# Two landmark inversions per batch joined into one chain, and projections whose row halves are swapped, in a Nyström attention and two FFN kernel

## The chip, the cores and the metric

One core of one Trainium2 chip runs the whole program. The metric is the device time of one execution in microseconds; of the kernel before, three runs were taken.

## The reference

Attention over 4 batches of 8 heads, 576 tokens, 64 wide; its output, 2304 tokens of 512, passes through two feed-forward layers (512 to 2048 to 512). All in fp32.

```
q_lm, k_lm = means of q, k over 18 neighbouring tokens     # 32 landmarks
A = sm(q, k_lm);  B = sm(q_lm, k_lm);  C = sm(q_lm, k)     # softmax of scaled products
Z = B.T / (max column sum of B * max row sum of B + 1e-6)
6 times: Z = 2 Z - Z B Z                                   # Newton steps
x = A Z C v
x = (h * tanh(softplus(h))) @ w_out,  h = x @ w_in         # layer 1, mish
x = silu(h) @ w_out2,                 h = x @ w_in2        # layer 2
```

## The kernel before

**Attention.** A group is four heads of one batch, so there are 8 groups, two to a batch. Per group, `sums` (L1074) and `main` (L1136) make the landmark means; `main` also makes B (128x32: four heads of 32 landmarks), its softmax, the two norms, and the first Newton product; `c_side` (L1304) makes C v; `a_side` (L1371) makes A with the landmarks on partitions (tile `at`, a high and a low part of 128x576, made by `at<-at,am`, an exponential, `at<-at,ar`, a transpose and a split); `newton` (L1258) carries the tile `yu` (32 columns of Y next to the 64 columns of u = C v) through six steps. In batch 0 a step is 8 matmuls of 32x32 blocks; from batch 1 on, a step first builds `bd`, a block-diagonal matrix, on DVE, then does `t<-yu,bd` on PE and `yu<-yu,t` on DVE. At its end `t<-bd,yu` gives Z C v, transposed, into `ut` (64 wide per head).

**Projections.** w_in of layer 1 isn't applied to the attention's output but folded into Z C v: `projection` (L641) multiplies `ut` of a batch with decoded columns of w_in (`wa`, 128x512) into `wp`. There are 16, four (`fb`, 512 columns each) per batch. One is 8 matmuls `t<-wa,ut` of 64 rows by 32 columns by 512, which the profile counts as 16 since an fp32 matmul has two records; then ACT or DVE copies the high part and DVE subtracts the low part (`wp<-t,wp`).

**Units.** Layer 1 then is 128 units of 6 matmuls `h<-at,wp` (128x288) and 12 `y<-g,wo` (L917, L946). Between them `gated` (L928) makes mish on ACT and DVE and splits it into a high and a low part (`g<-z,g`, 128x288). A unit needs `wp` and `at` of its batch (`h_time`, L1460).

**Weights.** They arrive in packed halves and `decode` (L530) restores fp32: one ACT pass, then a shift and two bit operations on DVE (`wa<-wst,wa`, `m<-wst,m`), then for w_out a high part and a low one (`wo<-m,wo`). Layer 2 works on three token tiles of 768 with seven products each (a Strassen scheme); `inputs` (L683) loads a tile's quarters and adds them on DVE (`wst<-wst`, 128x768).

**Order.** Nothing runs on its own: class `Line` is a planner that walks a clock of its own, with costs per engine, and records every instruction in the order in which it issues them (`issue`, L256; DMAs by SP in `transfer`, L268). Chains (generators) say which engine they want next; `KINDS` holds for each kind of chain a rank, a lead and a gap; `BIAS` shifts the choice where an operation may go to two engines (`split` for the low parts on DVE or POOL). If PE has nothing to do, `cold` (L188) lets the main loop put in fillers, transposes of `ident` whose results nobody reads. On the chip each engine then runs its list in that order and waits where data is late.

## Time and profile before

| | |
|---|---|
| median of 3 runs | 850.13 us (850.02 to 850.81) |
| profiled execution | 849.0 us, span 847.2 us |
| TensorE clock granted | 0.998 (2.4 GHz is 1) |
| first unit starts | 44.97 us |
| first projection of batch 1 | 123.91 us |
| layer 1 ends, layer 2 begins | 460.2 us |

The profile is that of one execution. Times in it count from the start of the span. PE is TensorE's matmuls, PEld its weight loads, DVE, ACT and POOL are the three other engines, SP issues DMAs. `out<-in` names tiles by the program's names without their numbers. The duration of a matmul includes its latency, so what one costs in a stream is the distance of starts.

### The profile page before, as it was taken

What the parts mean: (1) busy time and instruction counts of PE and PEld (TensorE: products, weight loads), DVE (VectorE), ACT (ScalarE), POOL (GpSimd) and SP (SyncE); (2) the same over time, 40 slices, a digit from 0 to 9 for tenths busy, and PEclk for the clock granted to TensorE, in tenths of its full rate; (3) what the DMA queues carried; (4) which work ended last, traced back from release to release, by engine and by line L of the source; (5) the groups of instructions that cost most, each with busy time, mean ns of one, the idle gap of its engine ahead of it and who ended that gap; (6) DMA issues with size and microseconds to landing.
All of it is one profiled execution on the core that took longest, in us unless ns stands there. A gap on an engine that the chain in (4) does not pass through costs nothing.

```text
span 847.2 us, 15580 instructions
## 1 busy us (share of the span) xinstructions
PE 828.9 (98%) x5922; PEld 735.2 (87%) x5922; DVE 532.3 (63%) x1088; ACT 445.1 (53%) x979; POOL 281.8 (33%) x324
## 2 busy tenths in 40 slices
PE   8999999999999999999999999999999999999997
PEld 6687978878899898989899898988888988998885
DVE  7968665664477787434407999877555567555542
ACT  6576765747465655433435665554444444544422
POOL 3323533442345565415333244221223221232210
PEclk9999999999999999999999999999999999999999
DMA  9664114200145465331117223101300000200002
GB/s 297 233 208 132 59 55 141 79 8 30 47 160 185 146 212 176 111 113 52 52 57 226 97 83 107 38 1 50 102 0 1 1 1 11 65 1 1 1 2 74
DMA packets 41483, 72.31 MB, mean 85 GB/s; under 512 B 4288, under 2 KB 30912, under 8 KB 41408
## 3 DMA queue, kind: packets, MB, share of 16 engines
q1 hardware_dynamic: 40832, 70.53, 26.1%
q8 instruction: 46, 0.75, 0.4%
q10 hardware_dynamic: 576, 0.79, 0.3%
q14 instruction: 29, 0.24, 0.1%
HBM read 57.15 MB, written 14.16 MB: 84 GB/s over the span
## 4 chain that ended last, share of the span: by engine, by line
PE 91%; DVE 3%; DMA 2%; ACT 2%; issue 1%; SPq 1%; DVEq 0%; ACTq 0%
PE y L256 49%; PE h L256 32%; PE t L256 10%; DMA wp<-in_q_dram 1%; SPq L268 1%; DVE z L256 0%; ACT z L256 0%; DMA wst<-ys 0%; DMA out_dram<-ysb 0%; DVE wa L256 0%; DVE at L256 0%; DVE nm L256 0%; ACT wp L256 0%; DVE asm L256 0%; ACT ysb L256 0%
## 5 line engine op out<-in xcount | busy, mean ns | idle before, releaser
L256 PE MATMUL y<-g,wo 128*128 128x288 f32 x1536 | 229.6, 300 | 0.0
L256 PEld LDWEIGHTS y<-g,wo 128*128 128x128 f32 x1536 | 209.0, 189 | 12.4 <-issue 11.3
L256 PE MATMUL y<-wo,xg 128*128 128x512 f32 x693 | 179.8, 395 | 0.0
L256 POOL TENSOR_TENSOR g<-z,g 128x288 fp32r<-128x288 f32 x127 | 112.7, 901 | 155.6 <-ACT g L256 114.5
L256 PEld LDWEIGHTS y<-wo,xg 128*128 128x128 f32 x693 | 128.6, 188 | 20.8
L256 DVE TENSOR_TENSOR z<-h,z 128x384 f32<-128x384 f32 x162 | 88.5, 554 | 67.6 <-PE h L256 65.0
L256 PE MATMUL h<-at,wp 128*128 128x288 f32 x768 | 120.8, 302 | 3.9 <-ACT z L256 3.7
L256 PEld LDWEIGHTS h<-at,wp 128*128 128x128 f32 x768 | 106.3, 188 | 12.1 <-ACT z L256 6.2
L256 ACT ACTIVATE z<-h 128x288 f32<-128x288 f32 x128 | 51.8, 413 | 70.4 <-PE h L256 65.6
L256 ACT ACTIVATE z<-z 128x384 f32<-128x384 f32 x94 | 49.4, 525 | 39.8 <-DVE z L256 39.4
L256 POOL TENSOR_TENSOR wo<-m,wo 128x512 fp32r<-128x512 f32 x32 | 47.3, 1480 | 47.6 <-ACT wo L256 39.6
L256 PE MATMUL h<-xg,wp 128*128 128x384 f32 x288 | 58.0, 336 | 1.5 <-DVE z L256 1.5
L256 PE MATMUL h<-xg,wf 128*128 128x384 f32 x288 | 57.7, 336 | 0.2 <-DVE z L256 0.2
L256 DVE TENSOR_TENSOR xg<-z,xg 128x384 fp32r<-128x384 f32 x75 | 43.2, 576 | 21.0 <-ACT xg L256 20.9
L256 DVE SCALAR_TENSOR_TENSOR m<-wst,m 128x512 int32<-128x512 int32 x64 | 55.4, 873 | 0.7
L256 PEld LDWEIGHTS h<-xg,wp 128*128 128x128 f32 x288 | 51.2, 188 | 5.1 <-DVE z L256 1.9
L256 PEld LDWEIGHTS h<-xg,wf 128*128 128x128 f32 x288 | 51.3, 188 | 3.6 <-DVE z L256 0.5
L256 ACT CAST g<-z 128x288 fp32r<-128x288 f32 x116 | 48.6, 435 | 8.7 <-PE y L256 7.5
L256 POOL TENSOR_TENSOR wf<-m,wf 128x256 fp32r<-128x256 f32 x20 | 15.2, 762 | 91.3 <-ACT wf L256 86.6
L256 PE MATMUL y<-wo,wp 128*128 128x512 f32 x171 | 44.9, 395 | 0.0
L256 DVE TENSOR_TENSOR wp<-t,wp 128x512 fp32r<-128x512 f32 x32 | 20.6, 685 | 33.6 <-ACT wp L256 33.6
L256 ACT ACT_TABLE_LOAD x31 | 39.8, 1283 | 3.3 <-PE h L256 2.0
(234 smaller groups left out, 1228.5 us busy)
## 6 DMA issues: line engine op xcount, KB each, us to landing
wst<-in_moe_w_out_dram SPq DMA_DIRECT2D x32, 512.0 KB, 6.0
wst<-in_moe_w_in_dram SPq DMA_DIRECT2D x28, 512.0 KB, 4.5
kn<-in_k_dram SPq DMA_DIRECT2D x8, 576.0 KB, 7.1
vn<-in_v_dram SPq DMA_DIRECT2D x8, 576.0 KB, 6.4
yh<-ysb SPq DMA_DIRECT2D x32, 144.0 KB, 1.8
ysb<-yh SPq DMA_DIRECT2D x32, 144.0 KB, 2.9
ys<-ysb SPq DMA_DIRECT2D x32, 144.0 KB, 2.2
qn<-in_q_dram SPq DMA_DIRECT2D x7, 576.0 KB, 4.8
```

The source lines that it names most:

```text
L256: r = getattr(self.nc[e], name)(**kw)
L268: return engine.dma_start(**kw)
```

## The change

Four things. (1) A class `Pair` does B's softmax, the norms and the Newton steps for both groups of a batch in one chain: tiles that were 128x32, 128x96 and 128x128 get a second half, and one DVE instruction does both groups; the matmuls stay per group. `Group.main` keeps only the means and is called `means`. The third and later groups may start before the Newton steps of the group two before are over; at an even group they wait for it. (2) In a projection, the second half of a batch (e = 1) keeps its row halves swapped, in `ut` (written so by the last product) and in `wa` (loaded so, by two DMAs of 64 rows). The eight matmuls then use all eight pairs of row half and output quadrant, where before they used four of them twice. The first projection and the decodes for it go in two halves of 256 columns, and units wait for `wp` per 128 columns. (3) The 128x768 sums of layer 2 go as two of 384. (4) The planner's constants change: ranks, biases (`split` from 1.0 to 0.2), 12 loads ahead instead of 6, and a rule (`HOLD`) by which lower chains and fillers stand back when a Newton chain is due on the engine within 0.5 us of the planner's clock.

Of `Group`, the lines of `main` behind the means and of `newton` go; the core of what is new:

```diff
-BIAS = dict(copy=0.6, split=1.0, scaled=0.1, x=0.2, x2=0.0, w_hi=0.5, w_lo=1.0)
+BIAS = dict(copy=0.8, split=0.2, scaled=0.1, x=0.2, x2=0.0, w_hi=0.35, w_lo=0.8)
...
-    M=(0, 0.6, 0.05),
-    F=(1, 0.3, 0.05),
+    M=(0, 1.5, 0.2),
+    F=(1.25, 1.5, 0.05),
     N=(2, 0.3, 0.05),
-    K=(2, 0.3, 0.05),
-    U=(2, 0.2, 0.05),
-    S=(2, 0.3, 0.05),
-    D=(3, 0.1, 0.2),
+    K=(3, 0.3, 0.05),
+    U=(3, 0.2, 0.05),
+    S=(2, 0.2, 0.05),
+    D=(2.5, 0.1, 0.2),
+    B=(2, 0.3, 0.05),
+    E=(1.25, 0.2, 0.05),
...
-LOADS, AHEAD = 6, 8
+LOADS, AHEAD = 12, 8
+HOLD, FIRST, APART, GATE, FILL, SIDE, SERIAL, LOPOOL = 0.5, 0, 2.0, 0, 0, "K", 1, 0
+SUMS = 3.9, 4.5
...
-        return self.now > 1.2 and self.free["T"] <= self.now and self.lately() < self.ENOUGH * 2.2
+        return self.now > 1.2 and not (HOLD and self.sooner("T", 3)) and self.free["T"] <= self.now and self.lately() < self.ENOUGH * 2.2
...
+    def kept(self, c):
+        return HOLD and c[6] and c[3] != "W" and self.sooner(c[3], KINDS[c[1]][0])
+    def sooner(self, e, rank):
+        at = max(self.now, self.free[e])
+        return any(
+            c[3] == e and KINDS[c[1]][0] < rank and not c[5] and c[0] <= at + HOLD and c[1] in "MFX"
+            for c in self.chains
...
-            due = [c for c in self.chains if self.start_of(c) <= self.now]
+            due = [c for c in self.chains if self.start_of(c) <= self.now and not self.kept(c)]
...
+        parts = 2 if o == "a" and f < KD else 1
+        for c in range(0, 512, 512 // parts):
+            if c:
+                yield from until(lambda: all(("a", 0, i, 0) in w_ready for i in range(KD)))
+                yield "A+"
+            n = slice(c, c + 512 // parts)
+            A.activation(out=f32(m[:, n]), in_=f32(a[:, n, 1]), func=ACTF.Copy, scale=2.0**-112)
+            yield "V+"
+            V.tensor_scalar(out=m[:, n], in0=m[:, n], scalar1=3, scalar2=None, op0=ALU.logical_shift_left)
...
+            V.scalar_tensor_tensor(
...
+            if c + 512 // parts < 512:
+                yield "A+"
...
+            elif o == "a" and kk >= KD // GB:
+                for e in range(2):
+                    to = a[64 * e:64 * e + 64].rearrange("p n t -> p (n t)")
+                    line.transfer(nc.sync, out=to, in_=src[64 - 64 * e:128 - 64 * e])
...
+        parts = 1 if fb or b else 2
+        n = FB // parts
+        yield from until(wp_r.any)
+        for c in range(0, FB, n):
+            done = [k if parts == 1 else (*k, c) for k in keys]
+            yield from until(lambda: all(w_ready.get(k, LATE) <= line.now for k in done))
+            yield from until(lambda: t_r.claim(GB))
+            pp = [t_r.take([128, FB], FP32) for e in range(GB)]
+            for i in range(HG):
+                for e in range(GB):
+                    r = slice(64 * ((i + e) % 2), 64 * ((i + e) % 2) + 64)
+                    T.matmul(
+                        out=pp[e][0][32 * i:32 * i + 32, 0:n],
+                        lhsT=ut_t[b][r, e, i // 2, :],
+                        rhs=f32(w_t[keys[2 * e + i // 2]])[r, c:c + n],
+                        start=True,
+                        stop=True,
+                    )
+            if not c:
+                wp_ = wp_t[b, fb] = wp_r.take([128, 2, GB, FB], F32R)
...
             for e in range(GB):
-                h = (i + e) % HG
...
-                    lhsT=ut_t[b][r, e, h // 2, :],
...
+                VA.copy(out=wp[:, 0, e, c:c + n], in_=pp[e][0][:, 0:n])
...
+            for f in range((fb * FB + c) // 128, (fb * FB + c + n) // 128):
+                wp_ready[b, f] = line.end + 0.12 + SLACK
...
-            VA.copy(out=wp[:, 0, e], in_=pp[e][0])
...
-            V.tensor_tensor(out=x12, in0=x22, in1=x12, op=ALU.subtract)
+            for k in range(2):
+                V.tensor_tensor(out=x12[:, k], in0=x22[:, k], in1=x12[:, k], op=ALU.subtract)
+                yield "V"
...
-        def main(self):
+        def means(self):
...
-                yield from until(marked((g, "Tk")))
+                yield from until(marked((g, "Tk"), (g, "Tq")))
...
-            yield from until(lambda: (g, "y") in marks and ("w", scr.name) in line.seen)
-            VAs.scaled(out=self.yu[:, LM:], in_=pu, scalar1=scr)
+            yield from until(lambda: ("w", scr.name) in line.seen)
...
+            line.add(self.means(), self.kind("N"))
+            line.add(self.c_side(), self.kind(SIDE), "W")
+            line.add(self.a_side(), "K" if self.g > 1 else "B")
...
+    class Pair:
...
             line.add(self.main(), self.kind("N"))
...
+        def main(self):
+            yield from until(marked(*((g, "lmT") for g in self.both)))
+            yield from until(self.banks.open)
+            pb_ = self.banks.take([128, GB, LM], FP32)
+            pb = pb_[0]
+            for i, g in enumerate(self.both):
+                lmT = groups[g].lmT
+                for h in range(HG):
+                    r = slice(64 * (h % 2), 64 * (h % 2) + 64)
+                    T.matmul(
+                        out=pb[32 * h:32 * h + 32, i, :],
+                        lhsT=lmT[r, 1, 32 * h:32 * h + 32],
+                        rhs=lmT[r, 0, 32 * h:32 * h + 32],
+                        start=True,
+                        stop=True,
+                    )
...
+            for i in range(GB):
+                A.activation(out=eb[:, i], in_=pb[:, i], func=ACTF.Exp, bias=nmb[:, i:i + 1], accum_out=sbm[:, i:i + 1])
...
+            V.tensor_tensor(out=bn, in0=eb, in1=bc(rb, LM), op=ALU.mult)
...
+            V.transpose(out=bt.rearrange("p g l -> p (g l)"), in_=bn.rearrange("p g l -> p (g l)"))
...
+            for i in range(GB):
+                self.each(py[0][:, i], bt[:, i], bt[:, i])
...
+            V.tensor_tensor(out=self.yu[:, :, 0:LM], in0=py[0], in1=bc(rc, LM), op=ALU.mult)
...
+            yield from until(marked(*((g, "u") for g in self.both)))
+            yield from self.newton()
...
+        def newton(self):
...
+            bd = s_p.tile([128, GB, HG, LM], FP32, tag="bd", name="bd", bufs=1)
+            whole = self.b > 0
+            for it in range(6):
+                lo = 0 if it < 5 else LM
+                if whole:
+                    yield "V"
+                    V.tensor_tensor(
+                        out=bd,
+                        in0=yu[:, :, 0:LM].rearrange("p g (o l) -> p g o l", o=1).to_broadcast([128, GB, HG, LM]),
+                        in1=mask.rearrange("p (o h) l -> p o h l", o=1).to_broadcast([128, GB, HG, LM]),
+                        op=ALU.mult,
+                    )
...
+                pn = self.banks.take([128, GB, LM + D], FP32)
+                for i in range(GB):
+                    if whole:
+                        T.matmul(
+                            out=pn[0][:, i, lo:],
+                            lhsT=bd[:, i].rearrange("p h l -> p (h l)"),
+                            rhs=yu[:, i, lo:],
+                            start=True,
+                            stop=True,
+                        )
+                    else:
+                        self.each(pn[0][:, i, lo:], yu[:, i, 0:LM], yu[:, i, lo:])
...
+                yn = s_p.tile([128, GB, LM + D], FP32, tag="yu", name="yu", bufs=3)
+                V.scalar_tensor_tensor(
+                    out=yn[:, :, lo:], in0=yu[:, :, lo:], scalar=2.0, in1=pn[0][:, :, lo:], op0=ALU.mult, op1=ALU.subtract
+                )
...
+                for g in self.both:
+                    marks.add((g, "step", it))
...
+            pu = self.banks.take([128, GB, HG // 2, LM], FP32)
...
+                    r = slice(64 * ((e + i) % 2), 64 * ((e + i) % 2) + 64)
+                    T.matmul(out=pu[0][r, i], lhsT=yu[:, i, LM:], rhs=bd[:, i, e::2], start=True, stop=True)
...
-                yield from until(marked((n - 1, "scores"), (n - 2, "done")))
+                yield from until(marked((n - 1, "scores"), (n - 2, "u"), (n - 2, "a_t")))
+                if n % GB == 0:
+                    yield from until(marked((n - 2, "done")))
...
-        return max([wp_ready.get((t // 2, f // 4), LATE)] + [a_ready.get((t // 2, e), LATE) for e in range(GB)])
+        return max([wp_ready.get((t // 2, f), LATE)] + [a_ready.get((t // 2, e), LATE) for e in range(GB)])
```

By these constants 120 of the 127 `g<-z,g` of POOL are now DVE's (POOL has 7), 29 of its 32 `wo<-m,wo`, and 7 of the 8 each of `at<-at,am` and `at<-at,ar`. Fillers go from 246 to 174: from 150 to 80 ahead of the first unit, and from 96 to 94 behind it. The order of the instructions at three places:

On PE, from the last Newton product to the first unit, before:

```order
L256 MATMUL h<-bd,yu 64x64 x2
L256 MATMUL t<-ident,kn 128x128 x3
L256 MATMUL t<-ident,qn 128x128 x3
L256 MATMUL y<-ident 128x128 x6
L256 MATMUL t<-wa,ut_141 32x512 x8
L256 MATMUL y<-ident 128x128 x26
L256 MATMUL t<-ident,qn 128x128 x3
L256 MATMUL t<-ident,kn 128x128 x3
L256 MATMUL y<-ident 128x128 x2
L256 MATMUL h<-at_629,wp 128x288 x8
```

and now:

```order
L262 MATMUL t<-bd,yu 64x64 x4
L262 MATMUL y<-ident 128x128 x4
L262 MATMUL t<-ident,kn 128x128 x3
L262 MATMUL y<-ident 128x128 x4
L262 MATMUL t<-wa,ut_141 32x256 x8
L262 MATMUL y<-ident 128x128 x8
L262 MATMUL t<-ident,kn 128x128 x3
L262 MATMUL t<-ident,qn 128x128 x3
L262 MATMUL y<-ident 128x128 x2
L262 MATMUL h<-at_633,wp 128x288 x2
```

The first projection has 256 columns and stands nearer to the first unit; fillers behind it are 10 instead of 28.

On PE, the end of batch 1's Newton steps and its first projection (`ut_142`), before:

```order
L256 MATMUL t<-yu,bd 128x96
L256 MATMUL y<-g,wo 128x288
L256 MATMUL t<-bd,yu 64x64 x2
L256 MATMUL y<-g,wo 128x288 x6
L256 MATMUL t<-wa,ut_142 32x512 x8
L256 MATMUL y<-g,wo 128x288 x8
```

and now:

```order
L262 MATMUL t<-yu,bd 128x96 x2
L262 MATMUL y<-g,wo 128x288 x12
L262 MATMUL t<-yu,bd 128x64 x2
L262 MATMUL y<-g,wo 128x288 x13
L262 MATMUL t<-bd,yu 64x64 x4
L262 MATMUL y<-g,wo 128x288 x7
L262 MATMUL t<-wa,ut_142 32x512 x8
```

Both groups' products stand side by side. Ahead of the projection stand 280 matmuls of units before (`h<-at,wp` and `y<-g,wo`), and 214 now.

On DVE, from the last Newton steps of batch 0 to the first `wp` (`m` are decodes of w_out, `aw_145` a buffer of w_in), before:

```order
L256 SCALAR_TENSOR_TENSOR yu<-yu,h 128x64
L256 TENSOR_SCALAR m<-m 128x512
L256 SCALAR_TENSOR_TENSOR bd<-bn,rc,mask 128x128
L256 SCALAR_TENSOR_TENSOR m<-wst,m 128x512 x2
L256 TENSOR_SCALAR m<-m 128x512
L256 SCALAR_TENSOR_TENSOR m<-wst,m 128x512 x2
L256 TENSOR_TENSOR wp<-t,wp 128x512 x2
```

and now:

```order
L262 STREAM_TRANSPOSE a_t<-at 128x576
L262 SCALAR_TENSOR_TENSOR bd<-bn,rc,mask 128x128 x2
L262 SCALAR_TENSOR_TENSOR wa<-aw_145,wa 128x256 x3
L262 TENSOR_TENSOR at_633<-a_t,at_633 128x576
L262 SCALAR_TENSOR_TENSOR wa<-aw_145,wa 128x256
L262 TENSOR_SCALAR m<-m 128x512
L262 TENSOR_SCALAR wa<-wa 128x256
L262 SCALAR_TENSOR_TENSOR m<-wst,m 128x512
L262 TENSOR_SCALAR wa<-wa 128x256 x2
L262 SCALAR_TENSOR_TENSOR wa<-aw_145,wa 128x256
L262 SCALAR_TENSOR_TENSOR wa<-wst,wa 128x256 x4
L262 TENSOR_TENSOR wp<-t,wp 128x256 x2
```

Of the w_out decodes, two instructions are left ahead of `wp`, where nine stood in all before; passes of `a_side` and second halves of w_in's decodes stand there now.

## Rows read from the trace of the kernel before

**Rows 1.** the page, part 1: busy time, share and instructions of each engine

```profile
PE 828.9 (98%) x5922; PEld 735.2 (87%) x5922; DVE 532.3 (63%) x1088; ACT 445.1 (53%) x979; POOL 281.8 (33%) x324
```

**Rows 2.** the page, part 4: the chain that ended last, by engine

```profile
PE 91%; DVE 3%; DMA 2%; ACT 2%; issue 1%; SPq 1%; DVEq 0%; ACTq 0%
```

**Rows 3.** busy time by stretch: PE, PEld, DVE, ACT, POOL; then the clock

```profile
0.00:44.97 44.97, 41.55 (x532) 31.26 (x533) 38.78 (x99) 25.12 (x63) 14.45 (x25) 1.00 0.76 250
...
42.73:126.50 83.77, 82.50 (x852) 70.29 (x851) 58.07 (x156) 59.00 (x116) 33.30 (x37) 1.00 0.36 115
```

**Rows 4.** the same view, DVE alone, later part of the start

```profile
13.82:44.97 31.15, 30.86 (x91) 1.00 0.68 242
```

**Rows 5.** timeline of DVE (start, duration, operation, tile), end of the start

```profile
36.69 0.21 DVE L256 SCALAR_TENSOR_TENSOR yu<-yu,h 128x64 f32<-128x64 f32 x1
...
37.42 2.37 DVE L256 SCALAR_TENSOR_TENSOR m<-wst,m 128x512 int32<-128x512 int32 x2
...
42.73 1.27 DVE L256 TENSOR_TENSOR wp<-t,wp 128x512 fp32r<-128x512 f32 x2
```

**Rows 6.** timeline of PE, the first projection and the first unit

```profile
39.42 1.93 PE L256 MATMUL t<-wa,ut 64*32 64x512 f32 x16
...
44.97 0.51 PE L256 MATMUL h<-at,wp 128*128 128x288 f32 x2
```

**Rows 7.** DVE groups by form, 13.82 to 42.73: count, busy, mean ns of one

```profile
L256 DVE SCALAR_TENSOR_TENSOR wa<-aw,wa 128x512 int32<-128x512 int32 x4 | 2.7, 676 | 0.0
...
L256 DVE TENSOR_TENSOR at<-a_t,at 128x576 fp32r<-128x576 f32 x2 | 1.5, 746 | 0.0
...
L256 DVE TENSOR_SCALAR m<-m 128x512 int32<-128x512 int32 x3 | 1.3, 418 | 0.2 <-ACT m L256 0.2
L256 DVE SCALAR_TENSOR_TENSOR yu<-yu,h 128x96 f32<-128x96 f32 x5 | 1.2, 240 | 0.0
```

**Rows 8.** DVE groups by form, whole span

```profile
L256 DVE TENSOR_TENSOR wp<-t,wp 128x512 fp32r<-128x512 f32 x32 | 20.6, 685 | 33.6 <-ACT wp L256 33.6
...
L256 DVE TENSOR_TENSOR ysb<-y,ysb 128x288 f32<-128x288 f32 x32 | 13.2, 456 | 43.8 <-PE y L256 43.7
...
L256 DVE TENSOR_TENSOR wp<-wi,wp 128x256 fp32r<-128x256 f32 x25 | 11.1, 444 | 10.0 <-ACT wp L256 9.9
```

**Rows 9.** PE groups by form, 44.97 to 460.2

```profile
L256 PE MATMUL y<-g,wo 128*128 128x288 f32 x1536 | 229.6, 300 | 0.0
```

**Rows 10.** timeline of one projection, PE and its weight loads (PEld)

```profile
184.04 1.93 PE L256 MATMUL t<-wa,ut 64*32 64x512 f32 x16
...
184.49 0.14 PEld L256 LDWEIGHTS t<-wa,ut 64*32 64x32 f32 x4 [0.29 <-issue]
184.92 0.14 PEld L256 LDWEIGHTS t<-wa,ut 64*32 64x32 f32 x4 [0.29 <-issue]
...
185.90 0.53 PE L256 MATMUL y<-g,wo 128*128 128x288 f32 x2
```

**Rows 11.** timeline of PE, one score product (8 matmuls of 64x32x288)

```profile
206.50 0.72 PE L256 MATMUL t<-Tq,lmT 64*32 64x288 f32 x16
207.14 0.53 PE L256 MATMUL y<-g,wo 128*128 128x288 f32 x2
```

**Rows 12.** timeline of PE, one small product among the units

```profile
96.32 0.26 PE L256 MATMUL t<-bt 32*32 32x32 f32 x8
96.52 1.32 PE L256 MATMUL y<-g,wo 128*128 128x288 f32 x8
```

**Rows 13.** what PE waited for, 44.97 to 460.2: total, times, longest

```profile
PE h L256 <- ACT z L256: 3.7, 6, 0.8
```

**Rows 14.** POOL groups by form, whole span

```profile
L256 POOL TENSOR_TENSOR g<-z,g 128x288 fp32r<-128x288 f32 x127 | 112.7, 901 | 155.6 <-ACT g L256 114.5 <-DVE g L256 14.4 <-PE h L256 14.2
```

**Rows 15.** timeline around one sum of layer 2, DVE and PE

```profile
602.63 1.08 DVE L256 TENSOR_TENSOR wst<-wst 128x768 f32<-128x768 f32 x1 [3.11 <-DMA wst<-ys]
...
604.70 1.31 PE L256 MATMUL h<-xg,wp 128*128 128x384 f32 x6 [1.49 <-DVE z L256]
```

More of the change, by code (lines that the diff above doesn't have):

```diff
@@ L270, in add @@
     def add(self, chain, rank, engine="W", ready=None):
-        self.chains.append([self.now if ready is None else ready, rank, next(self.count), engine, chain])
+        self.chains.append([self.now if ready is None else ready, rank, next(self.count), engine[0], chain, False, engine[1:]])
         return self.chains[-1]
@@ L280, in step @@
             return
+        c[5], c[6], engine = not self.end, engine[1:], engine[0]
         if not self.end:
@@ L642, in projection @@
         keys = [("a", 0, fb * KD + kk) for kk in range(KD)]
-        yield from until(lambda: wp_r.any() and all(w_ready.get(k, LATE) <= line.now for k in keys))
-        yield from until(lambda: t_r.claim(GB))
-        pp = [t_r.take([128, FB], FP32) for e in range(GB)]
-        for i in range(HG):
-            for e in range(GB):
-                h = (i + e) % HG
-                r = slice(64 * (h % 2), 64 * (h % 2) + 64)
-                T.matmul(
-                    out=pp[e][0][32 * h:32 * h + 32],
-                    lhsT=ut_t[b][r, e, h // 2, :],
-                    rhs=f32(w_t[keys[2 * e + h // 2]])[r, :],
-                    start=True,
-                    stop=True,
-                )
+        parts = 1 if fb or b else 2
@@ L657, in projection @@
         marks.add(("P", b, fb))
-        wp_ = wp_t[b, fb] = wp_r.take([128, 2, GB, FB], F32R)
-        wp = wp_[0]
-        yield "W"
-        for e in range(GB):
-            VA.copy(out=wp[:, 0, e], in_=pp[e][0])
-        yield "V"
-        for e in range(GB):
-            V.tensor_tensor(out=wp[:, 1, e], in0=pp[e][0], in1=f32(wp[:, 0, e]), op=ALU.subtract)
-            Ring.give(pp[e])
-        wp_ready[b, fb] = line.end + 0.12 + SLACK
-        yield "W"
     def split(out, of, lo):
@@ L721, in inputs @@
             yield "W"
[L722 removed]
+            for k in range(2):
+                V.tensor_tensor(out=x12[:, k], in0=x22[:, k], in1=x12[:, k], op=ALU.subtract)
+                yield "V"
             yield from until(lambda: "11" in issued)
[L724 removed]
+            for k in range(2):
+                V.tensor_tensor(out=x11[:, k], in0=x12[:, k], in1=x11[:, k], op=ALU.add)
+                yield "V"
             line.add(halves("s2", x11), "S", "W", line.end)
@@ L729, in inputs @@
             yield from until(lambda: "12" in issued)
-            V.tensor_tensor(out=x21, in0=x21, in1=x11, op=ALU.subtract)
+            for k in range(2):
+                V.tensor_tensor(out=x21[:, k], in0=x21[:, k], in1=x11[:, k], op=ALU.subtract)
+                yield "V"
             line.add(halves("22", x21), "S", "W", line.end)
@@ L734, in inputs @@
             yield from until(lambda: "s4" in issued)
-            V.tensor_tensor(out=x22, in0=x22, in1=x11, op=ALU.subtract)
+            for k in range(2):
+                V.tensor_tensor(out=x22[:, k], in0=x22[:, k], in1=x11[:, k], op=ALU.subtract)
+                yield "V"
             line.add(halves("s1", x22), "S", "W", line.end)
@@ L1170, in main @@
             marks.add((g, "lmT"))
-            yield from until(self.banks.open)
-            pb_ = self.banks.take([128, LM], FP32)
-            pb = pb_[0]
-            for h in range(HG):
-                e = h % 2
-                T.matmul(
-                    out=pb[32 * h:32 * h + 32, :],
-                    lhsT=lmT[64 * e:64 * e + 64, 1, 32 * h:32 * h + 32],
-                    rhs=lmT[64 * e:64 * e + 64, 0, 32 * h:32 * h + 32],
-                    start=True,
-                    stop=True,
-                )
@@ L1240, in each @@
-        @staticmethod
-        def each(out, lhsT, rhs, **kw):
-            for h in range(HG):
-                r = slice(32 * h, 32 * h + 32)
-                T.matmul(out=out[r], lhsT=lhsT[r], rhs=rhs[r], start=True, stop=True)
-        def blocks(self, y, by):
-            V.scalar_tensor_tensor(
-                out=self.bd,
-                in0=y.rearrange("p (o l) -> p o l", o=1).to_broadcast([128, HG, LM]),
-                scalar=by,
-                in1=mask,
-                op0=ALU.mult,
-                op1=ALU.mult,
-            )
@@ L1428, in attention @@
+    groups = []
     def attention():
-        groups = [Group(g) for g in range(NG)]
+        groups.extend(Group(g) for g in range(NG))
         for n in range(2):
@@ L1441, in attention @@
                 yield "W"
-                yield from until(marked((n - 1, "scores"), (n - 2, "done")))
+                yield from until(marked((n - 1, "scores"), (n - 2, "u"), (n - 2, "a_t")))
+                if n % GB == 0:
+                    yield from until(marked((n - 2, "done")))
+                if n < 4 and GATE:
+                    yield from until(marked(((1, "u"), (1, "y"), (0, "ut", 1), ("P", 0, 0))[GATE - 1]))
+            if n % GB == 0:
+                pair = Pair(n // GB)
+                pair.start()
+            groups[n].pair = pair
             groups[n].start()
@@ L1517 @@
         else:
-            if not grown and line.cold():
+            if not grown and (not FILL or (1, "step", FILL - 1) in marks) and line.cold():
                 for ring in (y_r, h_r, t_r):
```

257 lines of the change are left out of this document (125 added, 132 removed).

## The prediction

> **What bounds the kernel now.** I read the page first. PE is busy for 98% of the span, and the chain that ended last runs on PE for 91% [rows 1, 2]. So a change counts if it takes time out of PE's list, or out of the start, before units run. Of the start the page tells little, for fillers make PE look busy there. The view by stretches, for DVE alone, shows more: from 13.82 to 44.97 us DVE works for 30.86 of 31.15 us [rows 4]. DVE, not PE, sets when the first unit starts, since PE's list there is padded. Behind it, up to batch 1's first projection (42.73 to 126.50), DVE is busy for 58.07 of 83.77 us, or 69%, and PE for 82.50 [rows 3]. In all of layer 1 PE waits 3.7 us for ACT's `z`, and hardly for anything else [rows 13].
>
> The sum is made against the profiled execution of 849.0 us; the median of the runs shown stands 1.1 above it.
>
> **1. The start: -2.8.** DVE's queue up to the first `wp` is the measure, by the order of the instructions and by durations of rows; since neighbours overlap a little, I take about 0.07 off each. Gone ahead of `wp` are 2 shifts and 5 bit operations of w_out decodes, at 0.418 and, by the same operation on w_in, 0.676 [rows 7]: -3.7. The low part of `wp` has 256 columns, 0.444 each by a subtraction of that width instead of 0.685 [rows 8]: -0.5. Added are three passes of `a_side` that POOL did, priced by a DVE pass of the same 128x576 at 746 ns [rows 7]: +2.0; and two copies of `lmT`, +0.4. Two instructions of 240 ns [rows 7] become one of some 0.38, an estimate from its doubled width; over six steps and the softmax and norms that is -0.6. The 12 wide steps of the first w_in decodes become 24 of half the width, of which 20 stand ahead of `wp`; at an estimate of 0.27 and 0.41, between nothing and the wide rows, that is -0.4. Sum -2.8.
>
> The ends: the pair of decodes from 37.42 took 2.37 us [rows 5], against 2 x 0.676 undisturbed; if that stretch of 1.0 goes too, it is near -4. The other way: three loads for group 2 now go out on SP ahead of all of `aw_145` (the four DMAs of 64 rows), and its last load waits for group 0's C v. If the weights come late, DVE waits for them, and each link of the Newton chain is wider: +1.
>
> **2. Projections: -12.2.** One takes 1.86 us from its start to the next unit's matmul, in waves that start 0.43 apart, at 184.04, 184.49 and 184.92 [rows 10]; four waves of four records and 0.14 besides. A score product, also eight matmuls (16 records) of 64x32, uses all eight pairs of row half and output quadrant, and takes 0.64 for 288 columns [rows 11]: two waves of 0.43 x 288/512 = 0.24, and 0.16 besides. So a projection on eight distinct tiles takes two waves, 2 x 0.43 + 0.15 = 1.01 us. Fifteen of the 16 stand behind the start of the units: 15 x 0.85 = -12.8; the first one's second half now stands among units too, at 0.43 + 0.15 = +0.6. They lie on PE, which is full, so all of it counts. Ends: -12.8 to 0.
>
> Here the order of the loop says that the two halves of a wave write one bank from both row halves, while in a score product each bank has one row half only. That leaves a doubt. But in a projection of before, the four records that start together at 184.04 are the first of each of four tiles, and three of these, of e = 1, write one bank from both row halves. The Trainium skill has a rule against the change: TensorEngine Tiling (Array Packing), Gotcha 1: PSUM Pressure, says that different row tiles cannot access the same bank at a time. By it, the term would be 0; the row speaks against it. That the bank holds the two halves apart is rival B.
>
> **3. Joined small products: -1.5.** In batches 1 to 3, nine pairs of entries (`lmT`, `bt`, `bd,yu`) become one, and 18 pairs of Newton products. An entry costs PE 0.20 us by its distance to the next unit matmul [rows 12]. If a joined one costs what one did, nine save 1.8 to 2.2 and the steps up to 1; if it costs double, nothing: 0 to -3. I take the middle.
>
> **4. Units and waits: 0.** After the first unit, fillers are 94 instead of 96. But batch 1's first projection now stands after 214 unit matmuls instead of 280. At 229.6 us for 1536 [rows 9], 0.15 each, the stretch shrinks from 83.8 by 66 x 0.15 and by one shorter projection to about 73. In it DVE has more: 12 low parts of `g` (0.456 by a subtraction of 128x288, [rows 8]), 6 of `wo` at 0.68, 4 passes of `at` at 0.746 and seven more decode steps, less 14 narrow `bd`, 11 narrow `yu`, a landmark sum and small ones: +5. So 63 us in 73, 86%. The start shows that DVE can run at 99% [rows 4], so I take no wait; at worst, if its share stays at 69%, 63/0.69 = 91 us are needed: +18. POOL, which took 901 ns for each of 127 `g<-z,g` [rows 14], is relieved and bounds nothing.
>
> **5. Layer 2: 0.** The sum of 1.08 us starts when its DMA lands (3.11 us of idle DVE), and PE waits 1.49 behind it [rows 15]. Halves of the sum let a subtraction pass between; what waits for the DMA stays. Three such places, 0.5 either way.
>
> **Sum:** -2.8 - 12.2 - 1.5 = -16.5, so 832.5 for a profiled execution and **833.5** for the median.
>
> **Rivals.**
> A. *DVE turns into the bound of batch 1's approach.* For it: 86% needed against 69% seen, and PE's list is fixed, so what is late there makes PE wait. Against it: 99% in the start. With a share halfway, 77%, the stretch takes 63/0.775 = 81 us instead of 73: +8, 841.5.
> B. *The eight tiles don't run side by side,* because of the bank. Then all of term 2 is lost: 833.5 + 12.2 = 845.7. Against it is the wave at 184.04.
> C. *The clock falls in the start.* It stood at 1.00, the level of 2.4 GHz, in every stretch [rows 3], with 150 fillers ahead of the first unit; 80 are left. At 1.2 GHz most of PE's 41.55 us of the start wouldn't count, for it is padding. But some eight links of the chain, at 0.26 (as the small product of [rows 12]) to 0.4, and a projection of 0.58 would double: up to +4, 837.5. The Trainium skill, in TensorE: Matmul & The Clock Gate (What's actually happening), says that the default is the throttled state and activity releases it. No row of before shows a fall.
> D. *Slower: units wait for their own low parts.* A low part of `g` now stands in DVE's list, which runs in order, behind a decode of 0.68 or a wait for something late; PE's `y<-g,wo` then waits, where POOL had a lane of its own. If every third unit of 128 waits that long, 43 x 0.69 = 29 us: 862.5. It decides from 16.5/0.69, about 24 waiting units. Against it: up to five units are in flight between h and y (`FLIGHT`).
> E. *The change moves batch 1 forward in the list and all of that is gain:* 66 unit matmuls at 0.15 are 10 us, 823.5. Against it: PE is full there already, and a unit moved from ahead of the projection to behind it still has to run.
>
> **How the numbers follow.** Chances: forecast 0.64 (own range 828 to 838), A 0.17, B 0.06, C 0.05, D 0.04, E 0.04. The range leaves out D, B and the outer half of E: **825 to 844**. About 0.2% is what a measurement of this kernel can tell from no change: 848.4 to 851.8. Faster are all but D and the case where term 4's worst comes with an end of the others: 0.92; the same 0.03; slower 0.05.
>
> **What would show it.** Right: projections (`t<-wa,ut`, 16 records) at 1.0 us to the next matmul, in two waves; the first `h<-at,wp` at 42 us [rows 6]; batch 1's first projection at about 111; layer 1's end near 443; DVE at over 80% between; clock 1.00 throughout. Wrong: PE waiting for DVE's `g` or `yu` by more than some 3 us in layer 1, projections still at 1.8 us, or a granted clock under 1 before the first unit.

## The result, and the profile after

The changed kernel takes 836.9 us (median of 4, 834.75 to 837.07) against 850.08 for the kernel before: a ratio of 0.9841 (95% interval 0.9821 to 0.9861), 13.2 us less. The forecast of 833.5 was 3.4 too low; the range of 825 to 844 holds the time. The profiled execution took 836.9, its span 835.1. One of the four runs, 834.75, lies 2.2 below the other three, and only one execution was profiled.

I first asked where the time went. The view by stretches of the changed kernel (columns as in [rows 3]); the second row ends at batch 1's first projection, the third is layer 2:

```profile
0.00:40.05 40.05, 32.58 (x453) 23.77 (x454) 33.17 (x90) 19.69 (x52) 6.04 (x19) 0.96 0.86 280
40.05:106.28 66.23, 64.98 (x675) 56.76 (x673) 55.84 (x129) 41.73 (x89) 7.50 (x8) 1.00 0.44 127
444.76:835.10 390.34, 379.61 (x1874) 338.74 (x1872) 249.42 (x495) 188.35 (x405) 82.13 (x109) 0.99 0.13 39
```

The first unit starts at 40.05 instead of 44.97, batch 1's projection at 106.28 instead of 123.91, with DVE busy for 84% between (68% from 44.97 to 123.91 before), and POOL for 11%. Layer 1 ends at 444.76 instead of 460.2. Layer 2 takes 390.3, where it took 387.0.

A projection in the timeline of the changed kernel, PE and its weight loads, and behind it the next unit's matmul:

```profile
248.50 0.18 PEld L262 LDWEIGHTS t<-wa,ut 64*32 64x32 f32 x16 [0.17 <-issue]
248.50 1.09 PE L262 MATMUL t<-wa,ut 64*32 64x512 f32 x16
...
249.52 0.52 PE L262 MATMUL y<-g,wo 128*128 128x288 f32 x2
```

The weight loads of the kernel before, in the projection of [rows 10] and in the score product of [rows 11]:

```profile
184.03 0.17 PEld L256 LDWEIGHTS t<-wa,ut 64*32 64x32 f32 x8 [0.16 <-issue]
...
206.49 0.18 PEld L256 LDWEIGHTS t<-Tq,lmT 64*32 64x32 f32 x16 [0.16 <-issue]
```

All 16 weight loads now go at once, as in the score product, where before 8, 4 and 4 went at 184.03, 184.49 and 184.92. From a projection's start to the next matmul it is 1.02 us instead of 1.86.

What PE waited for from 40.05 to 444.75 (answers to [rows 13]):

```profile
PE h L262 <- ACT z L262: 4.0, 7, 0.8
PE t L262 <- DVE bd L262: 1.9, 3, 1.0
PE t L262 <- DVE at L262: 1.5, 1, 1.5
PE y L262 <- DVE g L262: 0.6, 1, 0.6
```

Before, the view had two lines besides the one for `z`:

```profile
PE t L256 <- ACT ec L256: 1.4, 2, 0.8
PE t L256 <- DVE yu L256: 0.3, 1, 0.3
```

So three of the four lines are new, 4.0 us in all, and two that came to 1.7 are gone: PE now waits for DVE in layer 1.

To hold the parts against the terms of the prediction, I took from the trace, for each matmul, the distance from its start to the next one's start, and summed these from the first unit to the end of layer 1 by kind. Layer 2 is here from its first to its last matmul. The same for every experiment, in us, each from its one profiled execution:

| kernel | first unit | projections | fillers | small products | units | end of layer 1 | layer 2 |
|---|---|---|---|---|---|---|---|
| before | 45.0 | 28.1 | 12.5 | 45.9 | 328.7 | 460.2 | 380.4 |
| changed | 40.1 | 16.3 | 11.1 | 44.7 | 332.6 | 444.8 | 383.1 |
| e1 swap alone | 44.8 | 15.4 | 12.5 | 45.9 | 331.1 | 449.8 | 379.0 |
| e3 no swap | 39.8 | 29.4 | 11.1 | 44.4 | 332.5 | 457.3 | 382.0 |
| e2 whole sums | 39.5 | 16.3 | 11.1 | 44.6 | 332.5 | 444.1 | 380.0 |
| e2b halves together | 39.9 | 16.3 | 11.1 | 44.7 | 332.7 | 444.7 | 380.2 |
| e5 fillers free | 38.8 | 16.4 | 17.6 | 45.1 | 331.0 | 448.9 | 379.4 |
| e6 low parts on POOL | 39.8 | 16.7 | 15.4 | 46.1 | 335.0 | 452.9 | 378.9 |
| e7 first projection whole | 46.1 | 17.5 | 11.1 | 45.0 | 330.4 | 450.1 | 379.2 |
| e8 swap and biases | 45.3 | 15.4 | 16.0 | 42.7 | 336.6 | 456.0 | 379.9 |
| e9 swap and first halves | 44.2 | 16.7 | 17.5 | 43.7 | 334.6 | 456.6 | 379.5 |
| e10 old constants | 44.9 | 22.7 | 14.4 | 45.5 | 329.7 | 457.2 | 379.5 |
| e11 no late fillers | 39.6 | 22.8 | 0 | 55.9 | 336.1 | 454.4 | 379.0 |
| e12 fewer fillers | 39.1 | 18.1 | 10.3 | 47.4 | 330.3 | 445.3 | 379.0 |

A wait of PE counts for the kind that stood before it. From before to changed: start -4.9, projections -11.8, small products -1.2, fillers -1.4, waits among units +4.0, layer 2 +2.6, and 0.7 more from the last matmul to the end (6.5 to 7.6 us in these kernels); together -12.1, the difference of the spans. A kernel's one profile can lie 1.5 to 2.7 us from its median: e3's was the fastest of its ten runs, e6's the fastest of four, e10's the slowest of four.

### The profile page after: what moved, and what is told of

The parts are those of the page before. It is cut to its first block, busy times and chain, and to the rows that moved or that the text cites. A ratio compares the mean times of both kernels' runs of the same rounds, so it can differ in the third digit from the quotient of the medians.

```text
span 835.1 us, 15221 instructions
## 1 busy us (share of the span) xinstructions
PE 808.3 (97%) x5866; PEld 723.9 (87%) x5866; DVE 555.8 (67%) x1193; ACT 432.8 (52%) x961; POOL 111.1 (13%) x154
## 4 chain that ended last, share of the span: by engine, by line
PE 86%; DVE 6%; ACT 3%; issue 2%; DMA 1%; SPq 0%; ACTq 0%; DVEq 0%
PE y L262 47%; PE h L262 31%; PE t L262 8%; DMA out_dram<-ysb 1%; ACT z L262 1%; ACT L262 1%; DVE wa L262 1%; DVE m L262 1%; ACT wp L262 1%; DVE z L262 1%; DVE at L262 0%; DMA kn<-in_k_dram 0%; DVE wo L262 0%; DVE wp L262 0%; DVE bd L262 0%
## 5 line engine op out<-in xcount | busy, mean ns | idle before, releaser
L262 PE MATMUL y<-g,wo 128*128 128x288 f32 x1536 | 226.1, 299 | 0.6 <-DVE g L262 0.6
L262 PE MATMUL h<-at,wp 128*128 128x288 f32 x768 | 122.6, 302 | 4.6 <-ACT z L262 4.0
L262 DVE TENSOR_TENSOR g<-z,g 128x288 fp32r<-128x288 f32 x121 | 53.9, 462 | 31.7 <-ACT g L262 28.6
L262 ACT CAST g<-z 128x288 fp32r<-128x288 f32 x122 | 50.8, 437 | 11.1 <-PE y L262 9.9
L262 DVE TENSOR_TENSOR xg<-z,xg 128x384 fp32r<-128x384 f32 x75 | 42.1, 561 | 20.4 <-ACT xg L262 20.3
L262 DVE SCALAR_TENSOR_TENSOR m<-wst,m 128x512 int32<-128x512 int32 x64 | 44.8, 704 | 0.7
L262 DVE TENSOR_TENSOR wp<-t,wp 128x512 fp32r<-128x512 f32 (+1 forms) x34 | 20.8, 655 | 29.6 <-ACT wp L262 29.6
L262 ACT CAST xg<-z 128x384 fp32r<-128x384 f32 x75 | 38.4, 513 | 1.5
L262 PEld LDWEIGHTS y<-wo,wp 128*128 128x128 f32 x171 | 31.7, 188 | 5.2
L262 POOL TENSOR_TENSOR wf<-m,wf 128x256 fp32r<-128x256 f32 x18 | 13.4, 743 | 171.4 <-ACT wf L262 169.7
```

The costliest lines, as they stand in the source:

```text
L262: r = getattr(self.nc[e], name)(**kw)
```

## Experiments

**The swap.** Alone on the kernel before, and taken out of the changed one. The order of PE's list stays as it is in both; that of SP's does not in e1, since two loads are split.

```diff
-                h = (i + e) % HG
-                r = slice(64 * (h % 2), 64 * (h % 2) + 64)
+                r = slice(64 * ((i + e) % 2), 64 * ((i + e) % 2) + 64)
...
-                    out=pp[e][0][32 * h:32 * h + 32],
+                    out=pp[e][0][32 * i:32 * i + 32],
```

(and the two loads of 64 rows, and `ut` written so; e3 is the reverse in the changed kernel.)

> The kernel before, with the swapped row halves of the projection alone; the order of PE's and DVE's instructions stays that of before. Theory 1 (the term of the prediction): each of 16 projections takes 1.02 instead of 1.86 us on PE; 15 of them lie among units, PE is full there, so all of it counts: 15 x 0.84 = 12.6, and the first one gives 0 to 0.84 more: 836.5 to 837.5. Rival: the list is fixed and other engines stay as they were, so part of the time comes back as PE waiting for DVE and ACT; with half of it back, about 843.

Measured: 836.43 (ratio 0.9851, 0.9837 to 0.9864), against 849.3 for the kernel before: -12.9.

> The changed kernel with the old rows and quadrants in the projection, all else kept, the order too. Theory 1: 15 projections by +0.84 and the two halves of the first by +0.4 each: +13, about 849.5. Rival: in the changed order PE waits 4 us more than before among units, so longer projections fill some of these waits: +9, about 846.

Measured: 849.51 (0.9997, 0.9988 to 1.0006). Both times fit theory 1 within 1 us. In e3's row of the table projections are 13.1 longer than in the changed kernel and no other column of layer 1 takes that back, so there the rival falls: projections lie on a full PE, and their time counts nearly whole. In e1 the sum hides two smaller things: projections are 12.7 shorter, units 2.4 longer (the view of waits has 1.2 us there for `g` that weren't in the kernel before), so a part came back as the rival said; and layer 2 is 1.4 shorter for another reason, the order of SP's list, which comes next. With e3 one more thing is shown that I had not asked: all else that the change does, without the swap, leaves the time of the kernel before.

**Layer 2's sums.** Here the third of layer 2's token tiles loads its last quarter (`wst<-ys`) while the first is stored (`out_dram<-ysb`) and PE works on the second. The changed kernel, timeline of SP, DVE and PE:

```profile
577.82 6.33 SPq L274 DMA_DIRECT2D out_dram<-ysb  x12
...
583.77 1.20 PE L262 MATMUL h<-xg,wf 128*128 128x384 f32 x6
584.25 0.38 SPq L274 DMA_DIRECT2D wst<-ys  x1
...
587.94 0.56 DVE L262 TENSOR_TENSOR wst<-wst 128x384 f32<-128x384 f32 x1 [4.24 <-DMA out_dram<-ysb]
588.42 0.42 DVE L262 TENSOR_TENSOR z<-wi 128x256 f32<-128x256 f32 x1
588.75 0.55 DVE L262 TENSOR_TENSOR wst<-wst 128x384 f32<-128x384 f32 x1
...
589.69 0.55 DVE L262 TENSOR_TENSOR z<-h,z 128x384 f32<-128x384 f32 x1
...
590.30 0.96 PE L262 MATMUL h<-xg,wp 128*128 128x384 f32 x4 [2.19 <-DVE z L262]
```

PE waits 2.19 us, where it waited 1.49 [rows 15]. It waits for `z<-h,z` (589.69), which stands behind the sum in DVE's list; the sum itself belongs to the next tile. DVE stands idle 4.24 us ahead of the sum. (The view names a store as what ended this; the sum reads what the load brings.) From the sum's start, which the landing sets, to PE's matmul it is 2.36 instead of 2.07 (602.63 to 604.70). And behind the wait the granted clock falls. The view by stretches of the changed kernel, PE alone, around the wait and behind it:

```profile
586.00:590.20 4.20, 2.11 (x11) 1.00 0.62 201
591.00:595.00 4.00, 4.00 (x14) 0.60 0.00 0
```

From the first matmul behind the wait to the 17th after it are 4.99 us instead of 3.42, so this costs 1.6. I made two versions, both edits of `inputs`:

```diff
-            for k in range(2):
-                V.tensor_tensor(out=x12[:, k], in0=x22[:, k], in1=x12[:, k], op=ALU.subtract)
-                yield "V"
+            V.tensor_tensor(out=x12, in0=x22, in1=x12, op=ALU.subtract)
```

(e2, so for all four sums; e2b takes out the `yield "V"` alone.)

> The changed kernel with layer 2's sums as one of 128x768 again. Theory 2: in the changed kernel a subtraction of 0.42 us stands between the two halves, so the chain from the landing of the DMA to PE's next matmul is 2.3 instead of 2.1 us, PE's wait 2.19 instead of 1.49, and behind this longer wait the clock falls to half for some 3 us, which costs 1.5. Whole sums bring the wait under 2 us and the clock stays at 1.00: -1.5 to -2.2, 834.7 to 835.4. Rival: the wait is longer since the DMA lands later against PE's own progress; then whole sums change 0.2 at most and the clock falls again: 836.5 to 837.

> The changed kernel with the halves of each layer 2 sum issued one right behind the other, so that nothing passes between. Theory 2 (the subtraction in between is the cause): as with whole sums, 834.7 to 835.4. Rival a (two halves cost more than one whole, whatever stands between): the wait stays above 2 us and the clock falls. Rival b (the DMA): 836.5 to 837, like the whole sums.

Measured: e2 833.88 (0.9822, 0.9809 to 0.9836), e2b 833.43 (0.9814, 0.98 to 0.9827). The times are those of theory 2 or better, but its reason doesn't hold. The same place in e2b:

```profile
577.81 5.07 SPq L274 DMA_DIRECT2D out_dram<-ysb  x8
...
582.98 0.38 SPq L274 DMA_DIRECT2D wst<-ys  x1
583.46 5.58 SPq L274 DMA_DIRECT2D out_dram<-ysb  x12
...
584.44 1.33 PE L262 MATMUL h<-xg,wf 128*128 128x384 f32 x6 [0.53 <-ACT z L262]
...
586.65 1.03 DVE L262 TENSOR_TENSOR wst<-wst 128x384 f32<-128x384 f32 x2 [1.67 <-DMA wst<-ys]
...
589.00 1.00 PEld L262 LDWEIGHTS h<-xg,wp 128*128 128x128 f32 x6 [0.52 <-DVE z L262]
589.00 1.31 PE L262 MATMUL h<-xg,wp 128*128 128x384 f32 x6
```

The chain from the sum to PE's matmul is still 2.35. But with the other order of steps the planner issues the load on SP behind 8 stores instead of 12, so it goes out 1.46 before the `h<-xg,wf` of 584.44 and not 0.48 behind the same matmuls, which start at 583.77 in the changed kernel. PE then waits in two shorter pieces (0.53 for ACT, 0.52 for DVE at the weight loads), and the clock stays at 1.00:

```profile
586.00:590.00 4.00, 3.92 (x20) 1.00 0.62 177
590.00:594.00 4.00, 4.00 (x21) 1.00 0.00 0
```

So the place of one load in SP's list, and the clock behind a wait of 2.2 us, are most of what costs in layer 2; the halves of the sum add 0.29 to the chain. That the kernel before also has the load behind 12 stores, and still waited only 1.49, fits: it went out as `h<-xg,wf` started (both at 598.87), 0.48 earlier against PE. And e3, which has the halves, the subtraction between them and the 12 stores as in the changed kernel, shows the timing alone: PE had waited 0.95 for ACT ahead of `h<-xg,wf`, the load went out 0.06 before it, and the wait behind the sum is 1.53, with no fall:

```profile
603.37 1.31 PE L262 MATMUL h<-xg,wp 128*128 128x384 f32 x6 [1.53 <-DVE z L262]
...
604.00:608.00 4.00, 4.00 (x21) 1.00 0.00 0
```

In the other eleven kernels the load stands behind 8 stores and goes out 1.46 to 2.15 ahead of `h<-xg,wf`; there the matmul at this place starts 0.23 to 0.47 after the one before it, so PE loses 0.24 there at most. e1 is one of them, and that, not the swapped rows, is its 1.4 in layer 2.

The length of a wait alone doesn't say whether the clock falls behind it. The longest wait of e6, with the clock behind it:

```profile
333.98 1.19 PE L262 MATMUL y<-g,wo 128*128 128x288 f32 x7 [2.40 <-DVE ysb L262]
334.00:338.00 4.00, 4.00 (x30) 1.00 0.66 162
```

Behind another one of 2.33 there, which ended at 278.86, the clock also stayed at 1.00 (279 to 283). In e9 a wait of 1.86 that ended at 335.98 was followed by 0.57 (336 to 340).

**The rest of the change.** From here on the changed kernel with halves together, 833.4, is the base. Each of these edits is a line or two, but the planner then orders everything anew, and the table's columns say what moved.

e5 lets fillers through whatever is due:

```diff
-        return self.now > 1.2 and not (HOLD and self.sooner("T", 3)) and self.free["T"] <= self.now and self.lately() < self.ENOUGH * 2.2
+        return self.now > 1.2 and self.free["T"] <= self.now and self.lately() < self.ENOUGH * 2.2
```

> The changed kernel with the halves of layer 2's sums together (833.4), and fillers no longer withheld when a Newton chain is near: 276 instead of 174, 132 of them ahead of the first unit instead of 80. In the changed kernel the granted clock falls to between 0.5 and 0.85 from 24 to 30 us. Theory C (the clock in the start costs time): with fillers the clock stays at 1.00 and the first unit comes 1 to 2 us earlier: 831.5 to 832.5. Theory DVE (DVE sets the start): the first unit moves by less than 0.5; but 50 more fillers behind the first unit stand in PE's fixed list, at 0.11 each up to 5.5 us: 833 to 839.

Measured: 837.22 (0.9856, 0.984 to 0.9872). The first unit is 1.1 earlier than in the base, more than theory DVE allowed, but 50 more fillers take 6.5 us more behind it, as it said. The clock isn't what moved the first unit: from 24 to 30 us it was 0.72 in the profile of the changed kernel, and 1.00 in the base, which has the same list there, and the first unit started at 40.05 and 39.95. What did move it here isn't shown.

e6 sets `split` back to 1.0:

> The changed kernel with the halves together, and the bias of low parts back at 1.0: all 128 low parts of g and all passes of at go to POOL, the joined chain and the projections stay. Theory (the relief of POOL pays, since beside POOL the passes of DVE are longer: 873 ns for a decode step in the kernel before, 704 now): slower by 2 to 4, 835.5 to 837.5. Rival (DVE is loaded too high in the approach to batch 1, and PE's 4 us of new waits among units come from there): these waits go, 830 to 832.

Measured: 842.79 (0.9918, 0.9894 to 0.9941), slower by 9.4. The theory had the sign, and too small a size. PE's waits went up, not down; lines of that view from layer 1:

```profile
PE h L262 <- ACT z L262: 8.5, 9, 2.3
PE y L262 <- DVE ysb L262: 2.4, 1, 2.4
...
PE t L262 <- DVE bd L262: 1.4, 4, 0.4
```

Fillers rose by 4.3 and units by 2.3. The lines for `at` and `g` are gone and `bd` is smaller, so these waits do hang on what DVE has to do; but the order that comes with the old bias has longer ones for `z` and `ysb` in their place. The mean of a decode step (`m<-wst,m`) on DVE is 798 ns again, with POOL busy for 243.3 us, as the theory's reason asks.

e7 makes the first projection and its decodes whole (`parts = 1` in both):

> The changed kernel with the halves together, and the first projection and its decodes whole. Theory (what the start gains is given back: the first unit is 4.9 us earlier, but by the 170th unit matmul the lead over the kernel before is gone and it is made up later by other parts): the first unit comes 1.5 to 2.5 later, the time stays within 1 us: 833 to 834.5. Rival (the start counts in full): 835 to 836.

Measured: 837.0 (0.9852, 0.9835 to 0.987): the rival, and more than it said. The first unit comes at 46.1, no earlier than in the kernel before, and 3.6 of the 6 us count in the end. A rival that I hadn't named is the clock: in e7's profile it stood at half in the start. PE of e7, and DVE of e7 and of the base from 13 us to the first unit:

```profile
28.00:41.00 13.00, 11.98 (x108) 0.50 0.77 289
```

```profile
13.00:46.10 33.10, 30.75 (x81) 0.79 0.71 233
13.00:39.95 26.95, 25.52 (x83) 1.00 0.84 281
```

DVE had 5.2 us more to do ahead of the first unit and was idle for only 0.9 more, so of the 6.15 us at most some 0.9 are the clock's, and the rest is DVE's list. The 3.6 at the end are less clean: from 444 to 448 the clock was 0.57 once more.

e8 and e9 put the biases, or the first halves, on the swap alone (e1):

> The kernel before with the swapped projections, and the new biases alone: 123 low parts of g go to DVE, the Newton chains stay one per group. Theory (joining the chains is what is worth the 3 us by which the changed kernel with halves together is ahead of the swap alone): 836 to 838. Rival (the relief of POOL is worth it): 833 to 834.

> The kernel before with the swapped projections and the first projection and its decodes in halves; the chains stay one per group, the constants as before. Theory 3 (the changed kernel's earlier start comes from the halves: with a whole first projection its first unit came at 46.1 instead of 39.95, and the time was 3.6 longer): the first unit comes 3 to 6 us earlier than 44.8, and the time is 832 to 834.5. Rival (the halves pay only beside the joined chain, as DVE's list ahead of the first wp is full with the two chains, or the gain comes back as fillers behind the first unit, of which there are 130 instead of 96): 836 to 838.

Measured: e8 844.64 (0.9944, 0.9925 to 0.9964), e9 846.0 (0.9974, 0.9956 to 0.9992). Each is slower than e1 by 8 to 10 us, more than either side had said. By the table, e8 has 3.5 more in fillers and 5.5 more in units, less 3.2 in small products; e9 has 4.9 more in fillers and 3.5 more in units, less 2.2. Each profile also has one fall of the clock in layer 1 (0.66 from 235 to 240 in e8, 0.57 from 336 to 340 in e9). In e9 DVE's low parts of `wp` are done at 42.1, but the first unit doesn't start. DVE, and then PE:

```profile
41.37 0.75 DVE L256 TENSOR_TENSOR wp<-t,wp 128x256 fp32r<-128x256 f32 x2
```

```profile
40.82 1.09 PE L256 MATMUL y<-ident 128*128 128x128 f32 x8
41.85 2.27 PE L256 MATMUL t<-Tk,twice 128*128 128x128 f32 x18
43.96 0.49 PE L256 MATMUL t<-ident,qn 128*128 128x128 f32 x3
44.20 1.29 PE L256 MATMUL h<-at,wp 128*128 128x288 f32 x8
```

PE's list has 18 products of the next groups' means ahead of it. What DVE gained there PE's fixed list gave away.

e10 keeps the structure and gives the planner the constants of before:

> The changed kernel's structure (joined chain, swapped projections, first halves, halves of the sums together) with the planner's constants of before: ranks, biases, 6 loads ahead, nothing held back; 282 fillers instead of 174, 120 behind the first unit instead of 94. Theory 4 (the structure and the constants belong together: with the old ones fillers and low parts on POOL come back, each of which cost 4 and 9 us when undone alone): 837 to 843. Rival (the joined chain pays by itself): 833 to 835.

Measured: 843.51 (0.9934, 0.9919 to 0.9948): theory 4's side, 0.5 above its range, and only in part for its reason. Fillers are up by 3.3, but in the table most of it is a start at 44.9 and projections of 22.7; PE stands in two of them for DVE, and the clock falls behind that (0.57 from 298 to 302):

```profile
292.35 1.07 PE L262 MATMUL t<-wa,ut 64*32 64x512 f32 x10
295.95 1.06 PE L262 MATMUL t<-wa,ut 64*32 64x512 f32 x6 [2.53 <-DVE wa L262]
298.41 2.55 PE L262 MATMUL t<-wa,ut 64*32 64x512 f32 x16 [1.41 <-DVE wp L262]
```

e11 and e12 take fillers away:

```diff
-            if not grown and (not FILL or (1, "step", FILL - 1) in marks) and line.cold():
+            if not grown and len(todo) == len(units) and (not FILL or (1, "step", FILL - 1) in marks) and line.cold():
```

(e12 instead changes the bound of `cold` from `self.ENOUGH * 2.2` to `self.ENOUGH * 1.5`.)

> The changed kernel with the halves of the sums together (833.4), and no fillers behind the first unit (80 in all instead of 174, the 80 ahead of it stay). They took 11.1 us of PE behind the first unit. Theory F1 (fillers stand where PE would wait for the attention of the next batch anyway; the 144 of the run with free fillers cost 3.8 us only since they were more than that): PE waits take their place, the time stays within 2 us of 833.4, unless the clock falls in the waits, which would add 1 to 3. Theory F2 (a fixed list makes PE run fillers even where the data is there already): 4 to 8 us faster, 825.5 to 829.5.

> The same kernel with the bound up to which fillers are given lowered: 118 in all, 66 ahead of the first unit and 52 behind it. F1: within 2 us of 833.4, the clock in the start somewhat lower. F2: half of the gain, 829 to 831.5.

Measured: e11 841.6 (0.9911, 0.9896 to 0.9925), e12 832.96 (0.9805, 0.9788 to 0.9821). Without late fillers PE waits in their place: small products and projections take 17.7 us more, fillers 11.1 less. And the clock falls three times in layer 1, each time where PE waits (from 72 us, with 0.50 from 127.8 to 134.6, and with 0.52 from 312 to 315); rows of the first, PE alone, by 6 us:

```profile
66.00:72.00 6.00, 4.82 (x58) 1.00 1.05 319
72.00:78.00 6.00, 3.70 (x29) 0.60 0.42 166
78.00:84.00 6.00, 6.00 (x62) 0.83 0.01 1
```

F1, with a higher price than it named: by these shares the clock stood at half for some 17 us, which can be up to 8 us of matmuls (an estimate), so what the waits alone cost isn't shown. Taking 42 of the 94 late fillers away (e12, with no fall in layer 1) makes no difference that can be told from the base: their intervals overlap. The 52 left stand for 10.3 us of PE, as a wait behind a filler counts for it, where 94 stood for 11.1. F2, which asked for 829 to 831.5, falls by that. e2b and e12 are the fastest versions run, some 3 to 4 us ahead of the changed kernel; e12's interval just touches the changed kernel's, e2b's still overlaps it a little.

## Why the prediction was right, and where it was not

**Term 2, projections, -12.2: right, and shown.** The 1.01 us worked out from two rows was 1.02 and a half 0.59; the sum is -11.8 in the trace, -12.7 in that of e1 (where the whole time fell by 12.9, with units 2.4 longer and layer 2 1.4 shorter), and 12.6 when taken out (e3, against the changed kernel). Rival B is out: that both row halves write one bank at once doesn't keep the eight tiles from running side by side. The rule of the Trainium skill (TensorEngine Tiling (Array Packing), Gotcha 1: PSUM Pressure) would have made the term 0; here the measurement differs from it.

**Term 1, the start, -2.8: the sign right, mis-sized,** -4.9 measured. DVE was busy 33.17 us ahead of the first unit instead of 38.78; the stretched pairs of decodes that I had put only into the lower end went too. e7 shows that it hangs on the first halves: without them DVE has 5.2 us more to do ahead of the first unit. What I left out of its working is that the lead needs PE's list to take it up: e9 has the halves and gets 0.6 of it.

**Term 3, joined small products, -1.5: the size right, half of the working not.** The table has -1.2, and the four tiles that were joined have -1.1 of it (10.7 to 9.6, waits included). All of that is the entries: a joined `lmT` or `bt` takes 0.26 to the next matmul instead of twice 0.20, and `bd,yu` 0.38 instead of twice 0.27. The Newton products, which I had put at up to -1, give nothing in sum (6.8 and 6.9): a joined one takes 0.36, two single ones 0.14 each, if a unit follows. The changed kernel, and the kernel before:

```profile
100.50 0.58 PE L262 MATMUL t<-yu,bd 128*128 128x96 f32 x4
100.87 0.90 PE L262 MATMUL y<-g,wo 128*128 128x288 f32 x5
```

```profile
117.66 0.36 PE L256 MATMUL t<-yu,bd 128*128 128x96 f32 x2
117.80 0.38 PE L256 MATMUL y<-g,wo 128*128 128x288 f32 x1
```

**Term 4, units and waits, 0: the step that failed first.** DVE's share was 84% where I had worked out 86%, so the pressure was seen rightly, and the time to batch 1 was even shorter than I had said (66 us for about 73). "I take no wait" was wrong: units +4.0 with fillers -1.4, so +2.6. The view of waits has the same net: 4.0 that are new (1.9 for `bd`, 1.5 for `at`, 0.6 for `g`) and 0.3 more for `z`, less the 1.7 for `ec` and `yu`, which the prediction's "hardly for anything else" had passed over. Only one of the new waits (1.04, for `bd`, ending at 96.34) lies in the stretch whose DVE load I had worked out; the others lie in later batches. It isn't rival A, since the approach to batch 1 became shorter; and not rival D: PE waited for `g` once.

**Term 5, layer 2, 0: the second.** "What waits for the DMA stays" held, but I took its place in time for fixed. The load went out 0.48 later against PE and the chain behind it was 0.29 longer, which made a wait of 2.19, and the clock fell behind it: +2.6 in all with smaller shifts at the layer's start. The cost of that clock was no part of the term. e2 and e2b gave 3.0 and 3.5 back.

**Rival C** happened in small: the clock fell to 0.72 from 24 to 30 us, where DVE sets the pace, and moved the first unit by 0.1 at most (40.05 against 39.95 with the same list). The cost of a lower clock came in layer 2, where I hadn't looked for it, behind 2.19 us of idle PE. The Trainium skill (TensorE: Matmul & The Clock Gate, What's actually happening) says that activity releases the throttle; the 0.60 behind that wait agrees.

**What the whole comes to.** The forecast promised 4.4 more than the spans show (-16.5 against -12.1), and that it came so near is in part luck: the start gave 2.1 more than its term and so hid a third of what terms 4 and 5 had left out. The swap alone gives 836.43, the whole change 836.9: their intervals overlap. The joined chain, the halves at the start and the constants are worth nothing measurable in the changed kernel, and some 3 us once layer 2 is mended (0.98 to 0.9827 against 0.9837 to 0.9864 for e1). The table says why: against e1, layer 1 ends 5.0 earlier, and layer 2 from its first to its last matmul is 4.1 longer, 2.8 of which e2b gives back. Taken singly they cost 8 to 10 us on the kernel with the swap (e8, e9), and taking one out of the whole costs 4 to 10 (e5, e6, e7, e10). Why a given set of constants puts a list together that fits and another doesn't I have only read case by case from the table; a rule for it stays open. So does what joining the two chains brings without the other parts, which I haven't run, and how much of the extra time of e6 to e11 the falls of the clock in their profiles are.

## What to carry to other kernels

If small fp32 matmuls of 64 rows by 32 columns run in waves of four, look at which pairs of row half and output quadrant they use: reordering the operands' halves, with no change in the amount of work, took 0.84 us off each of 15, and on a full PE nearly all of this counted (e3), or all but 2.4 of 12.7 us (e1). An edit that moves work in a list fixed beforehand is worth what the engine's list can take up, so price the wait behind the gained time, and test parts singly and together. And look at one load's place among stores in a DMA queue, and at what stands behind its reader in that engine's list, before blaming the arithmetic that waits for it.

## What the runs showed of the hardware that I had not expected

The clock fell to 0.60 over 4 us behind a wait of 2.19 us in layer 2, and not behind one of 1.49 in the kernel before; it cost 1.6 us, more than twice the growth of the wait. But it stayed at 1.00 behind 2.33 and 2.40 in e6, and was 0.57 behind 1.86 in e9. The same list in the start ran once at 0.72 (24 to 30 us) and once at 1.00, so a fall there isn't a property of the list alone. And the low parts of `g` cost DVE 462 ns each, where POOL took 901 [rows 14], while a decode step on DVE (`m<-wst,m`, 128x512) went from a mean of 873 to 704 ns when POOL's load fell from 281.8 to 111.1 us. Other kernels fall in line: 885 in e9 with 278.7, 798 in e6 with 243.3, 696 in e8 with 117.3. And eight fp32 matmuls of 64x32, the two row halves at once into one bank but each into its own output quadrant, take 1.02 us, not 1.86.
